# A new order for one core: DeltaNet attention and a GELU MLP, the same operations listed in another sequence

## The chip, the cores and the metric

The kernel runs on one core of a Trainium2 chip. The metric is the device time of one execution in microseconds, smaller being better. The five engines work through queues of their own: TensorE (PE; its weight loads are shown as PEld), VectorE (DVE), ScalarE (ACT), GpSimd (POOL) and SyncE (SP). SP computes nothing and issues most of the DMAs.

## The reference

A linear attention with the delta rule, over 4 batches and 8 heads with 768 tokens of 48 values, and a two-layer MLP on its output:

```python
k_n = k / (norm(k) + 1e-6)
for t in range(768):                       # per batch and head, state is 48x48
    y[t] = q[t] @ state
    v_old = k_n[t] @ state
    state = state + beta[t] * outer(k_n[t], v[t] - v_old)
x = y as (3072 tokens, 384)
h = x @ w_in                               # 384 -> 2048
out = gelu_tanh(h) @ w_out                 # 2048 -> 384
```

Inputs and outputs are float32; the kernel computes in bf16 with float32 sums.

## The kernel before

**Chunks.** The 768 tokens are cut into 12 chunks of 64 (c = 0 to 11). In a chunk the recurrence is a triangular system of 64 equations per batch and head, and its inverse is built by matrix products. A chunk has two units (u = 2c and 2c + 1), each of two batches on the two halves of the 128 partitions and 8 heads.

**Names.** Each operation is recorded by `A(engines, name, function, ...)` under a name such as `rt2.13`: the step, then the chunk or the unit.

- `load` (L422 to 433): k, q and v of a chunk by four DMAs each (`k5.01`), into one of three buffers; all but the first are on SP.
- `norms` (from L445): `sq`, `sum`, `pow`, `eps`, `nsq` or `nsa`, `inv`, `ib` give beta over the squared norm of k.
- `prep` (from L469), for a unit: `kc`, `kb`, `qb` cast and scale; their transposes come by PE and a copy (`T`, `kT`; in the first units `Tc`, `Tb`, `Tk`, `Tq`) or by a DMA transpose on SP (`turn`, L510). Gram matrices (`G2`, `G`; in the first units `GM`, `GQ`) are masked by DVE into `ln` and `wp` (L525). Then five rounds i = 1 to 5 double the precision of the inverse: `A_i` (8 products, L566), `rt_i` on DVE (add twice the identity, L578), `B_i` (8 products), and the copy of the result from PSUM into the block-diagonal operand `bd` of the next round. The sum may come from the identity matmul instead (`J`, `C`, with a copy `rj`). The copy to `bd` has three forms: two copies straight from PSUM (`bde`, L338), a copy and a masked copy that can follow each other at once (`bdf`, L338 and L344), or a copy to `xi` and two copies from there (`bdc`, L608, on POOL or DVE). `X10` and `X11` make the first operand (L555 on POOL, L557 on DVE).
- `chain` (from L611): `K`, `R`, `U`, `Un`, `S`, `Sn`, `Q`, `O`, `On` apply the inverse, carry the state to the next chunk and give the chunk's output. `X` with `xT`, or a DMA transpose `turnx` (L704), transposes the output for the MLP.
- `mlp` (from L708): 16 `up` of three matmuls each (L716), a `gelu` for each four of them (L720), 2 x 4 `down` of four matmuls each (L727), the copies `Z`, and the stores `out`.
- `weights` (L435 to 443): `w1.0`, `w1.1`, `w2.0`, `w2.1`, the halves of the two weight matrices, by DMAs that POOL issues, each released by the v loads of chunk 0. `w1.0` serves `up0` to `up7`, `w1.1` the others; `w2.0` serves `down00`, `down01`, `down10`, `down11`, `w2.1` the others.
- `warm_up`: 70 matmuls on zeros (`fill`), of which the order uses 31.

**What sets the order.** A string `ORDER` holds one sequence of all operations. A word gives the name, behind a colon the engine, where there is a choice (a, d, g, s), and behind an @ the PSUM bank that the operation takes. `Flow.order` hands each engine its words in that sequence, and `Flow.emit` puts semaphore waits in for the data and for the banks. So the string decides four things: which of the alternative forms is used, on which engine an operation runs, where it stands in that engine's queue, and in which bank a result lies. POOL operations on the two halves of the partitions also wait for each other.

A chunk's prep runs ahead of its chain, and the MLP of earlier chunks stands between on PE, a few matmuls at a time. In the order before, the four weight DMAs stand together:

```python
qb.1:g X11.1:g fill47@6 A1.0@7 rt1.0 fill52@6 Tk.2@6 kTk.2:d B1.0@3 C1.1 w1.0 w1.1 w2.0 w2.1 GM.3@6 GM.2@4 kTq.0:a bde11.0:a bde10.0:d C2.0
...
kb.4:g rt3.3 fill37@5 xT.0:a up0.0@0 B3.3@5 up4.0@2 up5.0 up6.0 up7.0 bde30.3:a bde31.3:a xi3.2:d A4.3@5 rt4.3 bdc30.2:g bdc31.2:g kb.5:g
```

Of the kernel before, what the change touches and what calls it, by code (L numbers as in the profile page):

```python
# [21 lines left out]
fill46@0 J1.1@0 fill22@1 fill64@2 Tc.1@1 fill12@2 betaT0@3 fill63@4 Tc.0@2 fill60@4 fill9@5 fill56@4 sq.0b:d sum.0a sum.0b tabS pow.0a
kTc.1:a betaA010 betaA001 pow.0b betaA011 betaA000 epsb:d eps.0a:d nsq.0a:g inv.0a eps.0b:d nsa.0b inv.0b triwpm0:d bdz0:d ib.0b:d triwpm2:d
upone0 sq.1:a sum.1 ib.0a:g kb.0:g bdz1:g kb.1:g betaT1@3 Tb.0@1 kTc.0:d betaN111 betaN110 Tb.1@4 fill25@2 kTb.0:a pow.1 eps.1:g nsa.1
kTb.1:d GM.0@6 GM.1@4 J2.0@2 fill16@1 betaN101 two:d betaN100 inv.1 ib.1:g kb.2:g ln.0 kb.3:d wpm.0 ln.1 ladj16:d wpm.1 qb.0:a fill36@3
# [4 lines left out]
X10.3:g bdc30.0:g X11.2:g qb.3:g bdf20.1:a bdf21.1:a C3.1 rj3.1:a A1.3@0 GQ.1@4 fill1@1 fill45@2 wqa.1 A4.0@1 B3.1@2 fill55@3 Tq.3@3 A1.2@4  # L30
fill41@5 rt4.0 sum.2 rt1.3 B4.0@1 wqa.0 bdf30.1:a bdf31.1:a A4.1@5 fill14@0 rt4.1 B4.1@5 fill20@0 bdf40.0:a rt1.2 pow.2 bdf41.0:a bde41.1:a
A5.0@2 B1.3@4 bde40.1:d rt5.0 kTq.3:d B1.2@0 bde10.3:a xi1.2:a R0a.0:d eps.2:g bdz5:g wqb.0 A5.1@5 B5.0@2 rt5.1 kc.4:d bde11.3:d B5.1@3
bdf50.0:a qb.2:a bdc11.2:g bdc10.2:g R0b.0:g Tq.2@5 A2.2@0 bde51.1:d rt2.2 wqb.1 nsq.2:g bde50.1:a bdf51.0:a A2.3@4 U.0@2 tabG Un.0:a rt2.3
# [4 lines left out]
gelu3.0 bdf50.3:a gelu2.0 bdf51.3:a kc.7:a down00.0@2 down01.0 sum.3 turn.5 X11.4:g wp.4 vs.1:d X10.4:d G2.5@0 S.0@6 A1.4@3 v2.01 v2.10
v2.11 q3.00 q3.01 q3.10 q3.11 k4.01 k4.10 k5.10 k4.00 k4.11 down02.0 ln.5 pow.3 eps.3:g nsq.3:g Sn.0:a bde50.2:a bde51.2:a rt1.4 inv.3 G.5@0
K.1@6 wp.5 X11.5:g X10.5:g ib.3:g kb.7:g R.1 qb.7:g B1.4@3 down10.0@4 down11.0 bde11.4:a bde10.4:a A1.5@5 GQ.2@0 A2.4@3 U.1@6 down03.0 rt1.5  # L40
rt2.4 Un.1:a wpq.2 B2.4@3 B1.5@5 xi2.4:a Q.1@6 S.1@0 O.1 down12.0 qb.6:g kb.6:g Z0.0:d bdc21.4:d bdc20.4:g A3.4@3 sq.4:g bdf10.5:a Sn.1
On.1:a turn.7 bdf11.5:a X.1@2 down13.0 xT.1:a rt3.4 sum.4 A2.5@5 B3.4@3 rt2.5 up0.1@6 up1.1 G.7@0 Z1.0:a bdf30.4:a bdf31.4:a B2.5@5 up2.1
A4.4@4 G2.7@2 up3.1 turn.6 q4.00 q4.10 q4.01 out11.0 q5.10 bde21.5:a bde20.5:a gelu0.1 wp.7 rt4.4 ln.7 up8.1@0 A3.5@5 B4.4@4 up9.1 G2.6@2
G.6@6 pow.4 eps.4:g rt3.5 ln.6 nsa.4 inv.4 ib.4:d wp.6 bdf40.4:a bdf41.4:a up10.1 B3.5@5 up11.1 up4.1@2 up5.1 A5.4@4 up6.1 bdf30.5:a
bdf31.5:a X11.7:g X10.7:g A4.5@5 A1.7@6 up7.1 X10.6:d rt5.4 X11.6:g kc.9:g q4.11 rt4.5 B5.4@7 A1.6@4 kb.8:g qb.8:g k5.11 v3.01 k5.00 k5.01
gelu2.1 kc.8:a gelu1.1 xi5.4:a v3.00 q5.01 turn.8 v4.01 v3.11 vs.2:g bdc51.4:g bdc50.4:g qb.9:g sq.5:g kb.9:g q5.11 k6.01 q5.00 turn.9 k6.00
k6.10 v3.10 k6.11 rt1.7 B4.5@5 up12.1@0 up13.1 up14.1 B1.7@2 rt1.6 B1.6@4 K.2@6 bde41.5:a bde40.5:d A5.5@5 down10.1@3 bde11.7:d rt5.5
bde11.6:a bde10.6:a bde10.7:a R.2 B5.5@5 A2.6@4 up15.1 A2.7@2 down00.1@6 bdf50.5:a bdf51.5:a gelu3.1 rt2.6 rt2.7 sum.5 B2.6@7 U.2@4
bdf20.6:a Un.2:a B2.7@2 bdf20.7:d down01.1 down11.1 bdf21.6:d bdf21.7:d down12.1 G2.8@4 Q.2@0 A3.7@2 ln.8 rt3.7 A3.6@7 O.2 On.2:a S.2@4
B3.7@2 pow.5 X11.8:g eps.5:g X10.8:g bde30.7:a bde31.7:a nsa.5 down02.1 G.8@0 rt3.6 B3.6@7 Sn.2 down03.1 bde31.6:a A4.7@2 X.2@4 wp.8 inv.5  # L50
rt4.7 A1.8@5 down13.1 rt1.8 Z0.1:a bde30.6:a xT.2:a B4.7@2 A4.6@7 Z1.1:d rt4.6 G2.9@0 G.9@4 ln.9 wp.9 B1.8@3 xi4.7:a qb.10:a ib.5:g kb.11:g
qb.11:g kc.10:d kb.10:g bdc41.7:g bdc40.7:g X11.9:g vs.3:g X10.9:g bdf10.8:a bdf11.8:a up8.2@6 B4.6@2 bde41.6:a bde40.6:a up9.2 up4.2@0
up10.2 up11.2 A5.7@4 gelu2.2 up5.2 up6.2 A5.6@5 sq.6:d rt5.6 rt5.7 sum.6 up7.2 up0.2@2 K.3@6 B5.7@4 B5.6@5 R.3 k7.01 k7.00 k7.10 out11.1
k7.11 q6.01 v4.11 turn.10 q6.10 out00.0 kc.12:g kc.11:g turn.11 sq.7:g gelu1.2 up1.2 A2.8@0 up2.2 A1.9@1 up3.2 up12.2@6 up13.2 bde50.7:d
rt2.8 rt1.9 bde51.7:a bdf50.6:a bdf51.6:a U.3@4 up14.2 B2.8@0 gelu0.2 Un.3:a B1.9@1 Q.3@2 up15.2 bde11.9:a bde21.8:a gelu3.2 pow.6 eps.6:g
nsq.6:g bde10.9:d sum.7 pow.7 kc.14:g bde20.8:a O.3 On.3:d inv.6 A2.9@1 down00.2@4 ib.6:d rt2.9 down01.2 G.10@2 G2.10@6 wp.10 ln.10 down02.2
B2.9@5 down10.2@1 A3.8@0 down11.2 G2.11@6 S.3@2 rt3.8 X11.10:g X10.10:g kb.12:g ln.11 bde20.9:a kc.13:a bde21.9:a B3.8@5 bdf30.8:a bdf31.8:a
kb.13:g X10.11:g X11.11:g A3.9@0 down12.2 down13.2 k8.00 q6.00 v4.10 q6.11 qb.12:a qb.13:g turnx.3 v4.00 k8.01 k8.11 turn.12 k8.10 rt3.9
Sn.3 A4.8@5 rt4.8 B3.9@0 A1.10@6 eps.7:g vs.4:g G.11@2 down03.2 wp.11 Z0.2:d rt1.10 Z1.2:a bdf30.9:a bdf31.9:a B4.8@5 bde41.8:a bde40.8:a
up12.3@0 up13.3 A1.11@2 A4.9@3 rt4.9 up14.3 up15.3 out11.2 q7.01 turn.13 q7.00 out00.2 v5.01 v5.10 v5.00 q7.11 v6.10 q7.10 v5.11 gelu3.3  # L60
rt1.11 up0.3@6 B1.10@3 B4.9@5 A5.8@4 up1.3 K.4@0 up2.3 up3.3 bde41.9:d rt5.8 R.4 bde40.9:a bdf10.10:a A5.9@2 bdf11.10:a up4.3@4 gelu0.3
# [729 lines left out]
```

## Time and profile before

| | before |
|---|---|
| median of 3 runs (lowest, highest) | 264.64 us (262.08, 266.8) |
| span of the profiled execution | 261.9 us |
| PE matmuls, busy | 5481, 243.3 us |
| DVE, busy | 346 instructions, 208.7 us |
| ACT, busy | 305 instructions, 189.7 us |
| POOL, busy | 216 instructions, 140.6 us |
| first `up` starts | 40.1 us |
| last `down` starts | 257.6 us |

The span runs from the first to the last instruction of the profiled execution; the times of the runs also hold what lies around it, and that execution's own device time is not listed apart from them. In the rows below, a group of instructions has its line, engine, operation, tiles and shapes, the count behind an x, then the busy time and the mean of one in ns, then the idle time of the engine ahead of them and what ended it. In the chain of waits a row has its start, its length, and the engine and line. A row of a window has its bounds and length, then for each engine the busy time and its count, then the granted clock of PE, the share of the DMA engines and the GB/s. Matmuls overlap and their ends are modelled, so the distance of starts tells PE's pace better than the busy time. Line numbers are those of the kernel before; behind the order string, those of the changed kernel are lower by 6.

### The profile page before, as it was taken

To read this page: it belongs to the slowest core of one execution; us is meant where nothing else is said; L and a number is where in the kernel's file an instruction comes from. 1 tells how busy PE (TensorE), PEld (TensorE's weight loads), DVE (VectorE), ACT (ScalarE), POOL (GpSimd) and SP (SyncE) were. 2 spreads that over 40 slices of the span, in tenths; PEclk is the share of its full clock that TensorE was granted. 3 is DMA by queue.
4 is the path that set the end of the run, shared out by engine and by line. 5 is a ranking of instruction groups with operands and counts; after the bars stand their busy time and mean duration, and the time that the engine had idled before them with its cause. 6 is when DMAs were issued, how large, how long until landed. Compare 5 with 4: busy or idle time off the path is not lost.

```text
span 261.9 us, 12280 instructions
## 1 busy us (share of the span) xinstructions
PE 243.3 (93%) x5481; PEld 189.0 (72%) x5481; DVE 208.7 (80%) x346; ACT 189.7 (72%) x305; POOL 140.6 (54%) x216
## 2 busy tenths in 40 slices
PE   5788869999999899979999989999999999999994
PEld 1356657777878768857887877787977878878672
DVE  4699996998999999949998979799999878665100
ACT  4878886879969867947986866887847858856260
POOL 7668563687986998575165462669433522011000
PEclk9979999999999999989999999999999999999999
DMA  4869999789986988993768969568976611001422
GB/s 89 148 128 154 194 186 179 139 158 170 151 154 131 139 158 159 161 166 72 142 121 161 175 122 149 102 121 111 161 144 86 120 33 33 5 3 33 91 64 60
DMA packets 118741, 31.87 MB, mean 122 GB/s; under 512 B 112800, under 2 KB 117920, under 8 KB 118688
## 3 DMA queue, kind: packets, MB, share of 16 engines
...
q0 software_dynamic: 2880, 3.15, 7.3%
...
## 4 chain that ended last, share of the span: by engine, by line
PE 75%; SPq 10%; DMA 6%; DVE 5%; issue 2%; ACT 1%
PE ps L727 24%; PE ps L716 21%; PE ps L566 18%; SPq L431 10%; DMA qraw<-in_q_dram 6%; PE ps L521 4%; PE ps L639 3%; PE ps L662 2%; PE ps L687 2%; DVE wp L525 1%; PE ps L674 1%; DVE sq L454 1%; DVE tok L484 1%; DVE rl L578 1%; SPq L406 0%
## 5 line engine op out<-in xcount | busy, mean ns | idle before, releaser
L716 PE MATMUL ps<-xT,W 128*128 128x256 bf16 x576 | 77.4, 273 | 0.4 <-ACT xT L338 0.2
L338 ACT ACTIVATE bd<-ps 64x512 bf16<-64x512 f32 x108 | 62.2, 588 | 17.6 <-PE ps L566 16.3
L727 PE MATMUL ps<-W,gT 128*128 128x384 bf16 x384 | 73.2, 329 | 0.0
L720 ACT ACTIVATE gT<-ps 128x1024 bf16<-128x1024 f32 x48 | 48.4, 1020 | 12.4 <-PE ps L716 12.0
L716 PEld LDWEIGHTS ps<-xT,W 128*128 128x128 bf16 x576 | 50.1, 98 | 6.4 <-ACT xT L338 0.5
L578 DVE TENSOR_TENSOR rt<-ps,two 128x512 bf16<-128x512 f32 x68 | 45.4, 684 | 6.6 <-PE ps L566 6.0
L727 PEld LDWEIGHTS ps<-W,gT 128*128 128x128 bf16 x384 | 33.7, 98 | 18.5 <-issue 0.7
L608 POOL COPY bd<-xi 64x256 f32<-64x256 f32 x46 | 19.0, 413 | 50.3 <-ACT xi L338 44.7
L555 POOL TENSOR_SCALAR_AFFINE_SELECT bd<-ln 64x512 bf16<-64x512 bf16 x43 | 29.7, 692 | 20.3 <-DVE ln L525 15.6
L525 DVE CAST_PREDICATED wp<-mup,ps 128x1024 bf16<-128x1024 uint16 (+1 forms) x26 | 28.3, 1090 | 2.6 <-PE ps L521 2.5
L457 POOL TENSOR_TENSOR nrm<-nrm,half 128x16 f32<-128x16 f32 x9 | 26.2, 2908 | 5.7 <-DVE nrm L455 5.5
L566 PE MATMUL ps<-rt,bd 128*128 128x64 bf16 x576 | 27.9, 194 | 0.3 <-DVE rt L578 0.3
L566 PE MATMUL ps<-wp,bd 128*128 128x64 bf16 (+1 forms) x576 | 27.3, 188 | 0.7 <-POOL bd L555 0.5
L578 DVE TENSOR_TENSOR rl<-ps,two 128x384 bf16<-128x384 f32 (+1 forms) x48 | 22.9, 483 | 5.4 <-PE ps L566 4.8
L338 DVE CAST bd<-ps 64x512 bf16<-64x512 f32 x37 | 25.0, 680 | 2.5 <-PE ps L566 2.1
L566 PEld LDWEIGHTS ps<-wp,bd 128*128 128x128 bf16 x576 | 23.6, 98 | 4.3 <-POOL bd L555 0.9
L566 PEld LDWEIGHTS ps<-rt,bd 128*128 128x128 bf16 x576 | 23.2, 98 | 4.2 <-DVE rt L578 0.8
L566 PE MATMUL ps<-rl,bd 128*128 128x64 bf16 x384 | 18.5, 193 | 2.1 <-DVE rl L578 2.1
L525 DVE CAST_PREDICATED ln<-mlo,ps 128x512 bf16<-128x512 uint16 x24 | 16.3, 682 | 4.9 <-PE ps L521 4.7
L566 PE MATMUL ps<-ln,bd 128*128 128x48 bf16 (+1 forms) x384 | 18.1, 188 | 1.0 <-DVE bd L338 1.0
L338 ACT ACTIVATE xi<-ps 128x512 bf16<-128x512 f32 x24 | 14.0, 593 | 6.5 <-PE ps L566 6.3
L566 PEld LDWEIGHTS ps<-rl,bd 128*128 128x128 bf16 x384 | 15.1, 98 | 4.8 <-DVE rl L578 3.1
...
## 6 DMA issues: line engine op xcount, KB each, us to landing
qraw<-in_q_dram SPq DMA_DIRECT2D x48, 96.0 KB, 3.4
vraw<-in_v_dram SPq DMA_DIRECT2D x48, 96.0 KB, 3.2
kraw<-in_k_dram SPq DMA_DIRECT2D x44, 96.0 KB, 3.3
...
W<-in_moe_w_in_dram POOLq DMA_DIRECT2D x2, 768.0 KB, 10.6
...
kT<-tok SPq DMA_TRANSPOSE x19, 4.5
out_dram<-ob SPq DMA_DIRECT2D x3, 96.0 KB, 2.1
```

Source lines behind the costliest of these rows:

```text
L338: return e.activation(out, in_, ACT.Copy) if e is nc.scalar else e.tensor_copy(out, in_)
L431: lambda e, P, n=n, a=a, y=y, xs=xs, view=view: e.dma_start(raw[n][s][hf(a), :, :].rearrange("p (xg y) d -> p xg y d", y=2)[:, xs, y, :], ...
L457: if e is nc.scalar else e.tensor_tensor(nr[:, 1, hx], nr[:, 0, hx], half[:, hx], ALU.pow), reads=[nrn, "half"] + ["one", "roots"] * (c < ...
L521: ins = e.matmul(o, kT[s][r, y, g, hf(a)], kT[s][r, z, g, hf(a)])
L525: return e.copy_predicated(out.rearrange("p (x g) t -> p x g t", x=2), mask[:, 0:wd].bitcast(U16).unsqueeze(1).unsqueeze(1).to_broadcast([ ...
L555: A(("pool", "dve"), op(f"X1{a}"), lambda e, P, src=ln[m][hf(a), :, :], dst=bd[b_][hf(a), :, hf(a)], a=a: e.affine_select(out=dst, in_=src ...
L566: ins = e.matmul(P(name)[:, C * h + cs.start:C * h + cs.stop], bd[b_][:, h, :], rhs[:, h, cs], **kw)
L578: A(("dve",), op(f"rt{i}"), lambda e, P, i=i, cs=cs, cn=cn, r_=r_: e.tensor_tensor(r_[:, :, cs], P(ps(f"A{i}")).rearrange("p (h t) -> p h ...
L608: A(("pool", "dve"), op(f"bdc{i}{a}"), lambda e, P, src=xi[i_][hf(a), :, :], dst=bd[b_][hf(a), :, hf(a)]: e.tensor_copy(dst.bitcast(F32), ...
L716: ins = e.matmul(P(ph)[:, 256 * f:256 * f + 256].rearrange("p (x t) -> p x t", x=2), W1[:, j, 128 * (i + f):128 * (i + f) + 128], x_[:, :, ...
L720: A(("act",), f"gelu{i // 4}.{c}", lambda e, P, i=i, ph=ph: e.activation(g_[:, i:i + 4, :], P(ph).rearrange("p (f t) -> p f t", f=4), ACT. ...
L727: ins = e.matmul(P(po)[:, 0:DM], g_[:, f, 128 * b:128 * b + 128], W2[:, f, :], start=(f == 0), stop=(f == FC - 1))
```

## The change

The order string is replaced by another one. Nothing else differs. The new string has 1735 words instead of 1750, since other alternatives are chosen in places; the words whose engine is the first of the possible ones carry no letter. On each engine the sequence is new from the first instruction on.

What the new string uses, in operations:

| step | before | after |
|---|---|---|
| copies `bde` on ACT, DVE | 78, 32 | 87, 27 |
| copies `bdf` on ACT, DVE | 56, 14 | 75, 17 |
| `xi` on ACT, DVE | 24, 6 | 14, 3 |
| `bdc` on POOL, DVE | 46, 14 | 29, 5 |
| `rt` on DVE, sums by `J` and `C` | 116, 4 | 119, 1 |
| `kb` on POOL, DVE | 19, 5 | 22, 2 |
| `vs` on POOL, DVE | 8, 3 | 10, 1 |
| `sq` on POOL, DVE, ACT | 5, 3, 5 | 6, 3, 4 |
| transposes of a unit by PE, by DMA | T.4, 19 | T.5 and T.10, 18 |
| transposes of a chunk's output by PE, by DMA | 5, 7 | 6, 6 |

The start, the places of the weights, and the first users of the weights, in the diff (the words on a line are in the one sequence):

```diff
-k0x0.10:s k0x0.01:s k0x1.01:s k0x1.10:s beta00:s k1.00 k1.01 k1.10 k1.11 beta11:s q0.00 q0.01 q0.10 q0.11 v0.00 v0.01 v0.10 v0.11 wz:d
-fill23@0 tmplz:d pad0:g pad4:g tmpl0 k0x0.00:a k0x1.00:a tmpl1 fill54@1 k2.00 k2.01 k2.10 k2.11 q1.00 q1.01 q1.10 q1.11 v1.00 v1.01 v1.10
...
-qb.1:g X11.1:g fill47@6 A1.0@7 rt1.0 fill52@6 Tk.2@6 kTk.2:d B1.0@3 C1.1 w1.0 w1.1 w2.0 w2.1 GM.3@6 GM.2@4 kTq.0:a bde11.0:a bde10.0:d C2.0
...
-gelu1.0 qb.5:g qb.4:a GQ.3@6 A4.2@4 rt4.2 up1.0 B4.3@5 up2.0 B4.2@4 up3.0 up12.0@2 wpq.3 bdf40.3:d bdf41.3:d bde40.2:a bde41.2:a T.4@6
...
+k1.00 bdz3:g upone0 one ident k0x1.00:a bdz0 pad1 wz:d fill16@1 mmup:d mup0 fill12@2 half:d fill36@3 fill65@0 k0x0.10:a mmlo:d k0x1.10 mlo0
+mlo1 k1.01 k0x1.11 k0x1.01 tmplz:d pad3:g tmpl0 tmpl1 identf triln0:g k0x0.11:a ident2 k0x0.00:a fill64@2 triln1:d fill66@0 ladj32:d
+fill52@6 fill22@1 k0x0.01:a upone1 fill28@3 bdz4 two fill49@0 beta00:a fill20@1 mup1 k1.10 beta01 k1.11 pad0:g sq.0b:d sum.0b beta10 pad4:g
...
+bde41.0 A5.0@0 rt5.0 kTq.0:a bdz2:g w1.1 B4.1@5 q4.00 bde40.1 X11.2 bde41.1:d X10.2 A1.2@4 rt1.2 B1.3@1 B5.0@0 GQ.0@6 A5.1@5 rt5.1 k3.01
+bde10.3 bdf50.0 bdf51.0 B1.2@2 bdf10.2 bdf11.2 fill47@3 k3.11 k4.00 bde11.3:d q3.01 qb.4:g B5.1@4 bde50.1 bde51.1:d w1.0 ib.2:g kb.4:g
+GQ.1@0 wpq.1 pad5:g R0b.0:g fill23@3 Tq.3@5 A2.2@2 rt2.2 A2.3@3 rt2.3 v1.11 kTq.3:a wqa.0 R0a.0:g U.0@0 Un.0 fill26@4 B2.2@2 bdf20.2:d w2.0
+B2.3@3 bdf20.3 bdf21.3 fill46@4 GQ.3@6 wqb.0 O.0@0 On.0 bdf21.2:d A3.2@4 rt3.2 kc.7:g A3.3@3 q4.11 rt3.3 X.0@2 xT.0:d B3.2@4 bde30.2:d
+bde31.2:d kc.5 B3.3@5 qb.5:a kc.6:g kb.5:g up4.0@2 up8.0@0 sq.3:g up5.0 up9.0 up10.0 up11.0 up6.0 bde31.3 wpq.3 bde30.3 A4.3@5 sum.3 up0.0@6
+up1.0 up2.0 tabG turn.4 q3.11 rt4.3 B4.3@5 v1.01 A4.2@4 up7.0 w2.1 gelu2.0 up12.0@0 up13.0 bdz5:g triwpm5:g bde41.3 pow.3 up3.0 rt4.2 B4.2@4
...
+A5.2@2 rt5.2 G.5@0 wp.5 vs.1 K.1@6 R.1 B1.4@4 bdf10.4 v3.01 down01.0 kb.7:g turn.7 X10.5 B5.2@2 bdf11.4 down02.0 GQ.2@0 A2.4@3 wpq.2 rt2.4
...
```

On SP's queue the loads no longer stand four by four: those of one chunk are spread, and loads of later chunks stand between. POOL's queue has kc.7, kc.6, kb.5 and sq.3 between w2.0 and w2.1.

More of the change, by code (lines that the diff above doesn't have):

```diff
@@ L22 @@
[L22 to L25, printed above, removed]
@@ L30 @@
[L30 to L33, printed above, removed]
@@ L38 @@
[L38 to L61, printed above, removed]
@@ new lines @@
+down10.0@4 X11.5 A1.5@0 v3.10 bde50.2 rt1.5 bde51.2 U.1@6 Un.1 sq.4:g sum.4 v3.11 down03.0 Z0.0 B2.4@3 bde20.4 B1.5@2 bdf10.5:d Q.1@6
+bde21.4 O.1 S.1@0 On.1 down11.0 q4.01 Sn.1 A3.4@3 rt3.4 kb.6:g turn.6 down12.0 bdf11.5 X.1@5 xT.1:d B3.4@3 A2.5@2 rt2.5 bde30.4 pow.4
+eps.4:g nsq.4:g inv.4 ib.4:g v2.11 bde31.4 G.7@0 kb.8:g G2.7@6 ln.7 X10.7 down13.0 Z1.0 B2.5@5 wp.7 up0.1@2 up4.1@6 bde21.5 bde20.5 A4.4@4
+k5.01 up1.1 up2.1 rt4.4 up3.1 G2.6@0 ln.6 A3.5@5 B4.4@4 rt3.5 X11.7 up5.1 up6.1 up7.1 qb.9:g kc.9:g gelu0.1 X11.6 B3.5@5 bde31.5 kb.9:g
@@ new lines @@
+X10.9 qb.11:g v4.00 X11.9 up9.2 up10.2 up11.2 gelu2.2 B1.8@1 xi1.8 bdc10.8 bdc11.8 A5.7@0 rt5.7 T.10@2 kT.10 A5.6@5 v5.01 B5.7@4 rt5.6
+A1.9@0 up0.2@6 up1.2 up2.2 up3.2 rt1.9 sum.6 A2.8@5 vs.4 kc.12 up12.2@0 B5.6@2 up13.2 up14.2 bdf50.7 bdf51.7 gelu0.2 qb.13:g bde50.6:d
+up15.2 bde51.6 out11.1 B1.9@4 out11.0 turn.11 G2.11@6 rt2.8 k7.00 sq.7:d gelu3.2 G2.10@2 ln.10 v6.00 ln.11 down10.2@5 bde10.9 U.3@0 Un.3
+B2.8@2 bde21.8:d down00.2@3 pow.6 bde11.9 k8.11 eps.6:g nsq.6:g Q.3@6 G.10@0 wp.10 O.3 On.3 A2.9@4 rt2.9 down01.2 down02.2 k8.01 bde20.8
@@ new lines @@
+q10.00 k11.00 B1.16@1 bdf10.16 bdf11.16 A5.14@0 rt5.14 v7.00 q10.10 rt1.17 B3.15@4 bde30.15 down01.5 down02.5 kb.18:g B5.14@5 bde51.14
+bde31.15 A2.16@7 down10.5@0 k10.00 sq.10:g sum.10 vs.7 B1.17@1 out00.3 R.7 down11.5 bde11.17 rt2.16 bde50.14 A4.15@2 bde10.17 rt4.15
+down03.5 out11.3 Z0.5:d q10.11 qb.20:a pow.10 B2.16@3 bde20.16:d out11.4 bde21.16 B4.15@2 down12.5 bde41.15 A2.17@1 rt2.17 down13.5 A3.16@3
+rt3.16 eps.10:g nsq.10 turn.18 G2.18@6 G.18@4 bde40.15 A5.15@1 rt5.15 wp.18 Z1.5 B2.17@0 bde21.17 up8.6@2 up9.6 B3.16@1 ln.18 turn.19 up10.6
@@ new lines @@
+A5.16@4 R.8 A1.19@0 A5.17@5 up12.7@6 rt5.16 B5.16@4 bde50.16 up13.7 up14.7 rt1.19 kb.21:g Z1.6 up15.7 gelu3.7 B1.19@0 rt5.17 B5.17@5
+bdf50.17 q11.00 q11.11 B2.18@1 xi2.18 up2.7 up3.7 qb.22:g bde51.16:d up8.7@6 up9.7 up10.7 turn.20 bdf10.19:d bdf11.19:d A2.19@4 kc.21
+turn.21 kc.22:g pow.11 up4.7@0 up11.7 v9.01 bdc21.18 bdf51.17:d bdc20.18:d A3.18@5 v11.00 up5.7 rt2.19 B2.19@4 gelu0.7 U.8@2 gelu2.7
+bdf20.19 eps.11:g rt3.18 B3.18@5 xi3.18 up6.7 up7.7 bdc30.18 Un.8:d v9.11 bdf21.19 v9.10 Q.8@6 nsq.11 G2.20@2 ln.20 bdc31.18 v10.11
```

130 lines of the change are left out of this document (67 added, 63 removed).

## Prediction

> **What bounds the kernel now.** I read the page's engine shares first, then the chain of waits in order of time, then the timeline around the two ends of the prologue, then the windows in which TensorE (PE) stood still.
>
> ```profile
> PE 243.3 (93%) x5481; PEld 189.0 (72%) x5481; DVE 208.7 (80%) x346; ACT 189.7 (72%) x305; POOL 140.6 (54%) x216
> PE 75%; SPq 10%; DMA 6%; DVE 5%; issue 2%; ACT 1%
> ```
>
> PE is busy 93% of the span and three quarters of the chain is PE. DVE at 80% is the only engine near it.
>
> ```profile
> 28.97 15.54 DMA qraw<-in_q_dram
> 44.53 0.53 ACT tok L338
> 45.20 0.83 PE ps L493 x12
> 59.27 0.51 PE ps L699 x6
> 95.18 0.76 PE ps L727 x4
> 96.17 0.65 PE ps L727 x4
> 112.58 1.71 issue
> 140.73 0.47 PE ps L566 x16
> 150.69 1.05 issue
> 248.00 5.24 PE ps L716 x48
> 253.24 5.21 PE ps L727 x32
> 258.48 0.49 ACT ob L338
> ```
>
> The last rows give PE's undisturbed pace: an up of 3 matmuls takes 5.24/16 = 0.328 us, a down of 4 takes 5.21/8 = 0.651, eight 128x128 products 0.47/2 = 0.235. The same down takes 0.76 where an operation in the other array mode (64-row tiles) follows it: a change of mode costs about 0.11.
>
> ```profile
> 40.08 0.50 PE L716 MATMUL ps<-xT,W 128*128 128x256 bf16 x3 [0.22 <-ACT xT L338]
> 50.00:60.00 10.00, 9.89 (x317) 7.28 (x315) 9.46 (x16) 8.29 (x15) 8.65 (x12) 1.00 0.92 153
> 113.00:114.00 1.00, 0.00 (x0) 0.00 (x0) 0.53 (x1) 0.00 (x0) 1.00 (x1) 1.00 0.85 146
> 116.00:117.00 1.00, 1.00 (x26) 0.57 (x18) 0.56 (x2) 0.69 (x2) 0.31 (x1) 0.50 0.75 146
> ```
>
> The first up starts at 40.08, so the span has three parts. Prologue: 40.08. From the first up to the end of the last down (258.48 less some 0.04): 218.4. Tail (copy, last store): 261.9 - 258.4 = 3.5. In the middle part PE's work, each operation at its pace, is 192 ups x 0.328 = 63.0, 96 downs x 0.65 = 62.4, 209 eight-matmul products 47.6, and 28.2 for Gram, state, output and transpose matmuls at the medians of their starts: 201.2. So about 17 us of the middle part is not work. Two stalls inside one operation, released by nothing the profile shows (1.71 and 1.05), belong to no order; after the first the granted clock was 0.50 for about 3 us, which costs half of that, 1.5. That is some 4.3; the remaining 13 are short waits on copies and DMAs.
>
> **The change, part by part.** Only the order string differs. I counted both queues operation by operation.
>
> PE. The first up in the new order is up4.0. The work from it to the end is that of before with one more 12-matmul transpose (T.5 and T.10 for T.4), one more 6-matmul transpose (X.5), one product and its neighbours less: 0.67 + 0.34 - 0.26 = +0.75. Mode changes go from 96 to 92: -0.4. Sum +0.35. Three identity matmuls in the prologue become DVE adds; they stood in idle time and cost nothing either way.
>
> Engines. The evacuation of a product now goes straight into the block diagonal (bde, bdf) more often, and by way of xi and two copies (bdc) less.
>
> ```profile
> L338 ACT ACTIVATE bd<-ps 64x512 bf16<-64x512 f32 x108 | 62.2, 588 | 17.6 <-PE ps L566 16.3
> L344 ACT ACTIVATE bd<-ps,up 128x512 bf16<-128x512 f32 x26 | 17.5, 673 | 0.0
> L338 ACT ACTIVATE xi<-ps 128x512 bf16<-128x512 f32 x24 | 14.0, 593 | 6.5 <-PE ps L566 6.3
> L608 POOL COPY bd<-xi 64x256 f32<-64x256 f32 x46 | 19.0, 413 | 50.3 <-ACT xi L338 44.7
> L608 DVE COPY bd<-xi 64x256 f32<-64x256 f32 x14 | 5.1, 363 | 1.1 <-ACT xi L338 0.8
> L484 DVE TENSOR_TENSOR tok<-kraw,nrm 128x384 bf16<-128x384 f32 x5 | 5.4, 1083 | 0.0
> L454 DVE TENSOR_TENSOR sq<-kraw 128x768 f32<-128x768 f32 x1 | 2.2, 2233 | 0.0
> L454 POOL TENSOR_TENSOR sq<-kraw 128x768 f32<-128x768 f32 x5 | 7.3, 1464 | 0.9 <-DMA kraw<-in_k_dram 0.7
> L338 POOL CAST tok<-kraw 128x384 bf16<-128x384 f32 x12 | 6.0, 502 | 2.7 <-DMA kraw<-in_k_dram 1.7 <-POOL bd L555 0.9
> L484 POOL TENSOR_TENSOR tok<-kraw,nrm 128x384 bf16<-128x384 f32 x19 | 16.2, 853 | 3.3 <-PE ps L674 2.8
> ```
>
> ACT: bd 108 to 123 (+8.8), bdf's second half 26 to 39 (+8.7), xi 24 to 14 (-5.9), smaller ones by their rows -6.7: +4.9. DVE: bdc 14 to 5 (-3.3), kb 5 to 2 (-3.2), whole squares 1 to 2 (+2.2), the rest -2.1: -6.4. POOL: bdc 46 to 29 (-7.0), against more scaling of k and v, casts and presets: about +2. All three stay under PE's 243. As PE ends last, I take these shifts at nothing; the cover is PE's queue, and in the stretch 50 to 60 above it is thin, DVE 9.46 of 10. For bare latencies I laid each PE operation at its pace and asked how late its producers come if no engine queues: the shortfalls over the middle part add up to 4.0 us before and 4.7 after. Neither order is tighter than the other in that.
>
> Prologue up to the first up. The first chunk's chain, walked in the new queues with the durations of the rows (transposes, Gram, five rounds of product, add, product, copy), reaches A1.0 at about 18.1 and U.0 at 35.2; before, they lie at 18.3 and 35.3. The last leg is one that can be followed:
>
> ```profile
> L338 ACT ACTIVATE us<-ps 128x768 bf16<-128x768 f32 x11 | 8.9, 807 | 1.4 <-PE ps L662 1.3
> L538 POOL TENSOR_TENSOR wp<-wp,mup 128x512 bf16<-128x512 bf16 x2 | 2.3, 1152 | 0.0
> L338 ACT ACTIVATE xo<-ps 128x768 bf16<-128x768 f32 x10 | 8.1, 808 | 10.8 <-PE ps L687 10.7
> L338 DVE COPY xT<-ps 128x768 bf16<-128x768 bf16 x2 | 1.1, 550 | 0.1
> ```
>
> ACT has kTq.3 and wqa.0 (0.6 each) between bde50.1 and Un.0, so Un.0 (0.81) ends at 37.1 and wqb.0 on POOL (1.15 from 36.3) at 37.5; then O.0. Two copies of unit 3 (0.59 + 0.67) come ahead of On.0 on ACT, which ends at 39.2; six transposes and xT.0, now on DVE (0.55), give 40.5 for the first up, against 40.1. The start is +0.4. ACT now issues all of the first half of k, one after another, but the second half, issued by SP, is squared first and covers it.
>
> Weights. This is the step that I think decides.
>
> ```profile
> 20.08 1.77 POOL L440 DMA_DIRECT2D W<-in_moe_w_in_dram  x2
> 21.85 1.78 POOL L442 DMA_DIRECT2D W<-in_moe_w_out_dram  x2
> 22.06 12.67 SPq L431 DMA_DIRECT2D qraw<-in_q_dram  x4
> 34.77 9.02 SPq L431 DMA_DIRECT2D kraw<-in_k_dram  x4
> DMA to landing us min/median/max: 9.0/14.4/21.4
> qraw<-in_q_dram SPq DMA_DIRECT2D x48, 96.0 KB, 3.4
> ```
>
> Before, POOL issues the four weight blocks in a row from 20.08; the first lands 9.0 later, the last 21.4 after its issue at about 22.8, at 44.2: after the first, one every (44.2 - 29.1)/3 = 5.0. While they move, loads on SP's queue take 12.67 and 9.02 for four instead of some 2.7, and the q of chunk 2 lands 15.54 after issue instead of 3.4. In the new order the blocks are spread over POOL's queue. By the same walk w1.1 is issued at about 27, w1.0 at 31 behind three mask steps, w2.0 at 34.6, w2.1 only behind kc.7, kc.6, kb.5 and sq.3 (0.50 + 0.50 + 0.85 + 1.46 = 3.3), and kc.7 waits for the k of chunk 3, which SP issues at about 27.7, into the weights. w1.0 should land at 27 + 9 + 4.2 = 40.2, just as the first up wants it: no cost. w2.0 lands at 45 to 46, before the first down at 40.5 + 8.1. For k of chunk 3 the bounds are the undisturbed 3.4 (landing 31) and the 15.54 of the q load among the weights (43.2). I take 42, nearer to the upper row, as two blocks are ahead of it. Then w2.1 is issued at 45.3 and, with the 9.0 of a block that finds the queue empty, lands at 54.3. Its first user, down02.0, stands 10.9 us of PE work behind the first up, and the Gram of chunk 2 before it waits for turn.4, a DMA transpose that SP issues behind the slowed loads. So down02.0 is due at 51.4 to 52: PE stands some 2.6 us. The bounds are 0 (k lands at 31) and 4.1 (k at 43.2, w2.1 at 55.5). Queued behind it are all later PE operations, so the stall is paid in full. What the change gives back, the q of chunk 2 ahead of the weights, saves only the 0.38 that PE waited there, and turn.4 takes it again.
>
> ```profile
> 45.20 0.83 PE L493 MATMUL ps<-ident,tok 128*128 128x128 bf16 x12 [0.38 <-ACT tok L338]
> ```
>
> A PE stall can cost more than itself: the 1.71 above was followed by a clock of 0.50 for 3 us, which would add 1.5 here; a wait of 1.05 was followed by none. I leave it out of the sum and in the range. The Trainium skill (TensorE: Matmul & The Clock Gate, Part 1: The HAM clock gate) says that the clock halves after at least one idle window of about 3.4 us; by it the stall costs 2.6 and no more, by the row 4.1. The trace speaks against the rule here.
>
> Sum: 261.9 + 0.35 (PE work) + 0.4 (start) + 2.6 (w2.1) = 265.3. The three timed runs have their median 2.7 above the profiled span, and I carry that over: 264.64 + 3.4 = **268.0**.
>
> **The rivals.**
> (a) Faster: DVE's queue, not PE, makes most of the 13 us of short waits. Its place is 50 to 110, where DVE is above 9 of 10. If all of the 6.4 us that it sheds comes out on the path and w2.1 comes in time, 264.64 + 0.75 - 6.4 = 259.0. It counts as faster only if over 5.3 + 0.75 of it comes out. Against it: only 5% of the chain is DVE. 0.13.
> (b) Slower by one mechanism, the weights: k of chunk 3 lands at the upper bound, w2.1 comes 4.1 us late, the clock halves (1.5), and the v of chunk 1, behind the same loads, is late by 2: 264.64 + 0.75 + 7.6 = 273.0. It decides from 4.6 us of stalls on. 0.23.
> (c) ACT becomes the bound in the middle: its 4.9 us come out on the path, on top of 3.4: 272.9. For it: ACT waits for PE in most of its idle time, so it is just in time; against it: 72% busy. 0.12.
> (d) The change does nothing that counts: weights and loads are hidden, 264.64 + 0.75 = 265.4. 0.14.
>
> **How the numbers follow.** The forecast as summed has 0.38. Faster by over 2% (below 259.3; 2% is about what a measurement of this kernel can tell from no change) is (a) with little else: 0.14. Slower by over 2% (above 269.9) is (b), part of (c), and the clock case of the forecast: 0.36. Within: 0.50. The range runs from (a) to a little beyond (b), 259 to 276; the forecast's own is 265 to 270.
>
> **What would show it.** Right: the first up at 39 to 42; w2.1 issued after 43; PE idle 1 to 4 us ahead of a down around 52, released by the landing of W; DVE busy near 202, ACT near 195; the middle part's other idle near 17. Wrong: no wait on W at all; short waits in 50 to 110 clearly fewer (a) or, on ACT's copies, more (c); a stall inside an operation of another length than 1.71, which no order explains.

## The result, and the profile after

The changed kernel takes 273.14 us (median of 4 runs, 270.21 to 275.92), the kernel before 264.73 (4 runs, 262.08 to 266.8): ratio 1.0305, 95% interval 1.0211 to 1.0399. It is slower. Medians here and below are of all runs, and ratios leave out the slow ones, those more than 1.5% above the quickest of the same kernel. The profiled execution took 270.21 us with a span of 268.5, the quickest of its four; the span before was 261.9. Line numbers after are 6 smaller than before.

Engine shares and the head of the chain, from the page of the changed kernel:

```profile
PE 244.6 (91%) x5490; PEld 191.1 (71%) x5496; DVE 197.6 (74%) x334; ACT 195.0 (73%) x315; POOL 140.5 (52%) x206
PE 66%; DMA 11%; SPq 7%; DVE 6%; POOL 5%; issue 2%; ACT 2%; POOLq 0%; ACTq 0%
```

PE's work is what it was, DVE is 11.1 us lighter, and PE's share of the chain has fallen from 75% to 66%: what grew is DMA, POOL and DVE. The chain of waits in order of time shows where:

```profile
26.41 0.64 SPq L425
27.08 13.79 DMA kraw<-in_k_dram
40.92 0.96 POOL tok L332 x2
41.88 0.79 POOL tok L478
42.67 1.44 POOL sq L448
44.13 0.95 DVE nrm L449
45.09 0.48 DVE rl L572
45.61 0.80 PE ps L560 x16
```

Read it from the bottom. PE starts B4.3 at 45.61, as soon as DVE has made rt4.3 (L572). DVE was free, but its queue had sum.3 (L449) ahead of rt4.3, and sum.3 reads sq.3, which POOL makes behind kc.7, kc.6 and kb.5, and kc.7 reads the k of chunk 3, whose last load takes 13.79 us where such a load takes 3.4 by the median. The timeline of the changed kernel has the three engines standing one behind another (start, length, engine, in brackets the idle time before and what ended it):

```profile
40.92 0.96 POOL L332 CAST tok<-kraw 128x384 bf16<-128x384 f32 x2 [5.71 <-DMA kraw<-in_k_dram]
44.04 0.94 POOL L436 DMA_DIRECT2D W<-in_moe_w_out_dram  x1
...
44.13 0.95 DVE L449 TENSOR_REDUCE nrm<-sq 128x16 f32<-128x768 f32 x1 [2.52 <-POOL sq L448]
...
45.61 0.48 PE L560 MATMUL ps<-rl,bd 128*128 128x64 bf16 x8 [2.33 <-DVE rl L572]
...
88.35 0.53 PE L515 MATMUL ps<-kT 48*64 48x64 bf16 x16 [0.98 <-DMA kT<-tok]
98.43 0.49 PE L515 MATMUL ps<-kT 48*64 48x64 bf16 x32 [1.81 <-DMA kT<-tok]
```

The last two rows are a second loss, at Gram matrices that wait for DMA transposes (turn.9 and turn.11). The windows (PE's busy time first, the granted clock third from the end) hold both, first the changed kernel, then the kernel before:

```profile
40.00:58.00 18.00, 15.21 (x307) 11.54 (x304) 11.59 (x19) 12.37 (x19) 14.82 (x20) 0.91 1.13 162
78.00:98.00 20.00, 17.15 (x422) 14.12 (x420) 15.51 (x24) 16.38 (x27) 15.12 (x18) 1.00 0.88 150
...
45.00:47.00 2.00, 1.39 (x20) 1.19 (x21) 1.10 (x4) 0.59 (x1) 2.00 (x3) 0.70 0.64 129
47.00:49.00 2.00, 2.00 (x15) 1.41 (x13) 0.59 (x2) 1.02 (x1) 1.97 (x1) 0.50 1.35 210
49.00:50.00 1.00, 1.00 (x27) 1.00 (x25) 0.40 (x1) 0.99 (x2) 0.42 (x2) 0.90 1.28 192
```

```profile
40.00:58.00 18.00, 17.54 (x476) 13.97 (x476) 15.32 (x25) 13.57 (x22) 10.96 (x17) 1.00 0.90 153
78.00:98.00 20.00, 19.05 (x475) 14.91 (x475) 19.12 (x28) 16.88 (x28) 17.21 (x22) 1.00 0.84 144
```

The wait of 2.33 is followed by some 3.4 us at half the clock (that is what 0.70, 0.50 and 0.90 in the three short windows add up to), and PE does 307 matmuls in the first stretch where it did 476. To put sizes to this I took each PE operation's start to the next one's start, less the pace of its kind in the trace of before, and summed the rest by stretch (us):

| | before | after | after_small_w | clear_of_weights | clear_and_v3_early |
|---|---|---|---|---|---|
| first up starts | 40.08 | 39.62 | 37.96 | 39.88 | 40.54 |
| lost, 40 to 60 | 1.7 | 6.1 | 2.3 | 3.0 | 3.2 |
| lost, 60 to 80 | 1.6 | 1.2 | 1.3 | 1.5 | 1.7 |
| lost, 80 to 110 | 2.7 | 7.0 | 3.9 | 4.7 | 2.0 |
| lost, 110 to 160 | 7.8 | 4.8 | 4.2 | 5.0 | 4.7 |
| lost, from 160 | 2.9 | 3.7 | 4.6 | 3.7 | 3.9 |
| last `down` starts | 257.63 | 263.76 | 255.49 | 259.89 | 257.87 |

(The three columns on the right are kernels of the next section.) The 6.1 us between the first two columns is +4.4 early, +4.3 at 80 to 110, +0.5 of work (what the losses leave of the time behind the first up) and +0.4 elsewhere, less 0.5 at the start and 3.0 at 110 to 160, where the kernel before has its two stalls inside an operation and the half clock.

### The profile page after: what moved, and what is told of

Same layout as the page of the kernel before. It is cut to its first block, busy times and chain, and to the rows that moved or that the text cites. A ratio compares the mean times of both kernels' runs of the same rounds, so it can differ in the third digit from the quotient of the medians.

```text
span 268.5 us, 12276 instructions
## 1 busy us (share of the span) xinstructions
PE 244.6 (91%) x5490; PEld 191.1 (71%) x5496; DVE 197.6 (74%) x334; ACT 195.0 (73%) x315; POOL 140.5 (52%) x206
## 3 DMA queue, kind: packets, MB, share of 16 engines
q1 hardware_dynamic: 111584, 26.90, 57.5%
q0 software_dynamic: 2880, 3.15, 7.0%
## 4 chain that ended last, share of the span: by engine, by line
PE 66%; DMA 11%; SPq 7%; DVE 6%; POOL 5%; issue 2%; ACT 2%; POOLq 0%; ACTq 0%
PE ps L721 20%; PE ps L710 19%; PE ps L560 15%; DMA kraw<-in_k_dram 8%; SPq L425 6%; PE ps L515 3%; PE ps L633 3%; DMA kT<-tok 2%; PE ps L681 1%; PE ps L656 1%; DVE wp L519 1%; DVE ln L519 1%; DMA vraw<-in_v_dram 1%; POOL nrm L451 1%; DVE nrm L449 1%
## 5 line engine op out<-in xcount | busy, mean ns | idle before, releaser
L332 ACT ACTIVATE bd<-ps 64x512 bf16<-64x512 f32 x123 | 71.6, 588 | 26.1 <-PE ps L560 24.2
L721 PE MATMUL ps<-W,gT 128*128 128x384 bf16 x384 | 74.2, 328 | 0.4 <-issue 0.4
L710 PEld LDWEIGHTS ps<-xT,W 128*128 128x128 bf16 x576 | 51.5, 99 | 7.5 <-issue 0.6
L572 DVE TENSOR_TENSOR rt<-ps,two 128x512 bf16<-128x512 f32 x71 | 48.1, 685 | 10.1 <-PE ps L560 9.6
L549 POOL TENSOR_SCALAR_AFFINE_SELECT bd<-ln 64x512 bf16<-64x512 bf16 x41 | 27.2, 662 | 25.2 <-DVE ln L519 21.9
L572 DVE TENSOR_TENSOR rl<-ps,two 128x384 bf16<-128x384 f32 (+1 forms) x48 | 23.0, 484 | 9.2 <-PE ps L560 8.6
L338 ACT ACTIVATE bd<-ps,up 128x512 bf16<-128x512 f32 x39 | 26.1, 674 | 2.0 <-DVE bd L332 2.0
L560 PEld LDWEIGHTS ps<-wp,bd 128*128 128x128 bf16 x576 | 21.8, 97 | 6.3 <-DVE wp L519 2.3
L602 POOL COPY bd<-xi 64x256 f32<-64x256 f32 x29 | 11.7, 406 | 25.1 <-ACT xi L332 21.8
L478 POOL TENSOR_TENSOR tok<-kraw,nrm 128x384 bf16<-128x384 f32 x22 | 18.1, 830 | 4.5 <-DVE nrm L460 3.0
L560 PEld LDWEIGHTS ps<-rl,bd 128*128 128x128 bf16 x384 | 16.1, 99 | 5.3 <-DVE rl L572 3.0
```

The lines of the kernel that those rows point to most:

```text
L332: return e.activation(out, in_, ACT.Copy) if e is nc.scalar else e.tensor_copy(out, in_)
L338: return e.activation(out, in_, ACT.Copy, scale=up1[:, 0:1]) if e is nc.scalar else e.tensor_scalar(out, in_, up1[:, 0:1], None, op0=ALU.mult)
L478: A(("dve", "pool"), op("kb"), lambda e, P: e.tensor_tensor(kb, kr, nr[:, 5, hx].unsqueeze(2).to_broadcast(full), ALU.mult), reads=[f"kraw ...
L549: A(("pool", "dve"), op(f"X1{a}"), lambda e, P, src=ln[m][hf(a), :, :], dst=bd[b_][hf(a), :, hf(a)], a=a: e.affine_select(out=dst, in_=src ...
L560: ins = e.matmul(P(name)[:, C * h + cs.start:C * h + cs.stop], bd[b_][:, h, :], rhs[:, h, cs], **kw)
L572: A(("dve",), op(f"rt{i}"), lambda e, P, i=i, cs=cs, cn=cn, r_=r_: e.tensor_tensor(r_[:, :, cs], P(ps(f"A{i}")).rearrange("p (h t) -> p h ...
```

## The experiments

Each edit only moves words of the order string, except where said. Times are medians, ratios are to the kernel before on the same chip.

**First round: the two places in the trace.** Theory one: the weights' traffic delays k of chunk 3, and DVE's queue passes that on. Theory two: from 56 us on SP issues loads with 20 us and more to spare ahead of DMA transposes. Rival: the new forms and engines, or PE's order.

k3_early, on SP's queue:

```diff
-k3.00 q2.00 q3.10 v2.00 q2.10 q3.00 v1.10 k3.10 q4.00 k3.01 k3.11 k4.00
+k3.00 k3.01 k3.10 k3.11 q2.00 q3.10 v2.00 q2.10 q3.00 v1.10 q4.00 k4.00
```

> The changed kernel with one edit: the other three k loads of chunk 3 (k3.01, k3.10, k3.11) stand right behind k3.00 on SP's queue, ahead of q2.00, so that they are on their way before the first weight block. Theory of the weights: kc.7 no longer waits 5.7 us on POOL, sq.3 and sum.3 come before rt4.3 is due, the 2.6 us gap of PE ahead of B4.3 at 42.7 and the half clock behind it go, w2.1 is issued before 40; time 4 us below the changed kernel's 273.1, so about 269, ratio to the kernel before 1.015. Theory of SP's queue (its order from 56 us on is the loss): less than 1.5 us, about 272, ratio 1.03, since the transposes of 83 to 98 us come as late as before. Theory of the forms and engines (more copies on ACT): no change, 273, ratio 1.03.

273.97 us, ratio 1.0367 (1.0293 to 1.0442): nothing gained. The wait ahead of B4.3 is gone, but q2.10 now goes out 0.3 us behind the first weight block and takes 9.5 us, and POOL stands for it, with w1.0 and the scaled v of the first chain behind it; PE waits 7.01 us for that in U.0, and the first up starts at 45.04. POOL's row and PE's, in k3_early:

```profile
35.12 0.50 POOL L332 CAST tok<-qraw 128x384 bf16<-128x384 f32 x1 [7.03 <-DMA qraw<-in_q_dram]
...
39.35 0.82 PE L656 MATMUL ps<-rs,bd 128*128 128x48 bf16 x16 [7.01 <-POOL rs L638]
```

sum3_late, the sequence cut to the words that count (bde41.3 runs on ACT, pow.3 on POOL):

```diff
-sum.3 rt4.3 bde41.3 pow.3 rt4.2
+rt4.3 bde41.3 rt4.2 sum.3 pow.3
```

> The changed kernel with one edit: sum.3 and pow.3 stand behind rt4.3 and rt4.2 on DVE's queue instead of ahead of them; loads, weights and all else stay. Theory of the weights, if DVE's queue standing behind sum.3 is what PE pays: rt4.3 runs as soon as A4.3 is done, the gap of 2.3 us ahead of B4.3 goes or shrinks below 0.8, though k of chunk 3 still lands at about 41; 269 to 271. If the lateness of k itself is what costs (v of chunk 1, k of chunk 4, w2.1 behind it): the gap goes but the time comes back before down02.0 at 56, 272 to 273. Theory of SP's queue and theory of the engines: under 1 us, 272 to 273.

270.28 us, ratio 1.0246 (1.0182 to 1.0309). The wait ahead of B4.3 goes, as theory one says of DVE's queue, and comes back one operation later. Timeline of sum3_late, POOL, DVE, PE:

```profile
43.61 0.95 POOL L332 CAST tok<-kraw 128x384 bf16<-128x384 f32 x2 [8.55 <-DMA kraw<-in_k_dram]
...
46.81 0.95 DVE L449 TENSOR_REDUCE nrm<-sq 128x16 f32<-128x768 f32 x1 [2.33 <-POOL sq L448]
...
48.41 0.36 PE L560 MATMUL ps<-wp,bd 128*128 128x32 bf16 x8 [2.98 <-DVE bd L332]
```

The time hits the 269 to 271 of theory one, but the wait that was to go has only moved, and the interval overlaps that of the changed kernel, so no gain is shown. A word moved on one queue only changes who is behind the late load.

sp_by_need and k3_early_sp_by_need: all that SP issues after 52 us in the order of first use, alone and with k3_early. On SP's queue, the part around turn.9:

```diff
-turn.8 k6.10 q6.11 v4.01 k6.11 q5.11 q5.01 k7.01 out00.0 v3.00 q6.01 turn.9
+v3.01 turn.8 v3.10 v3.11 v3.00 turn.9 v4.10 v4.01 v4.11 v4.00 q6.10 q6.11
```

> The changed kernel with one edit: the DMAs that SP issues after 52 us in the changed kernel's trace are put in the order of their first use there (a DMA transpose 2 us sooner), so that turn.8, turn.9 and turn.11 no longer stand behind loads and stores that have 20 to 40 us to spare. Theory of SP's queue: PE's waits on the DMA transposes (2.8 us by the trace's groups) go and the bubbles of PE between 80 and 110 us fall from 7.0 to about 3; time 4 us below 273.1, about 269, ratio 1.015. Theory of the weights: the 42.7 us gap stays and the later waits are only its echo, so less than 1 us, 272 to 273. Theory of the engines: 273.

> The changed kernel with both edits, the k loads of chunk 3 ahead of the weights and SP's queue by need from 52 us on. If both theories hold and add up: 273.1 - 8 = 265, ratio 1.00. If the weights alone: 269. If SP's queue alone: 269. If the forms and engines or PE's own order are what costs: 272 or more, ratio 1.03.

275.66 us, ratio 1.0439 (1.0367 to 1.0512), and 274.89, ratio 1.0404 (1.0318 to 1.0489). Neither gains. In the first, k of chunk 3 lands later still and B4.3 waits 5.27; the wait on turn.9 is gone, but turnx.3, put only 2 us ahead of its need, makes PE wait 2.49, and a wait of 2.12 on a transpose at 100 stays. In the second nothing waits for k, and PE stands for turn.4 instead, the DMA transpose of unit 4, which is issued among the weights:

```profile
52.00 0.43 PE L515 MATMUL ps<-kT 48*64 48x64 bf16 x16 [5.54 <-DMA kT<-tok]
...
41.97 7.77 SPq L504 DMA_TRANSPOSE kT<-tok  x1
```

So the single-load form of theory one falls: in these traces, whichever load is caught among the weights, something early needs it.

**Second round: take the traffic away.** after_small_w and before_small_w load one block of 128 for each half of the two matrices and let all ups and downs read it, so that seven eighths of the weights are left out of the computation:

```diff
-e.dma_start(W1[:, :, f0:f0 + FF // 2], w1v[:, :, f0:f0 + FF // 2])
+e.dma_start(W1[:, :, f0:f0 + 128], w1v[:, :, f0:f0 + 128])
-e.dma_start(W2[:, n0:n0 + FC // 2, :], w2v[:, n0:n0 + FC // 2, :])
+e.dma_start(W2[:, n0:n0 + 1, :], w2v[:, n0:n0 + 1, :])
-W1[:, j, 128 * (i + f):128 * (i + f) + 128]
+W1[:, j, 1024 * (i // 8):1024 * (i // 8) + 128]
-W2[:, f, :]
+W2[:, f // 8 * 8, :]
```

> The changed kernel with an eighth of the weights: each half of the two matrices loads one block of 128 (one row block of the second matrix) and all its ups and downs read that one, so that TensorE does the same matmuls and seven eighths of the weight traffic are left out. The computation is changed in that. Theory that the weight traffic and what it delays is the whole loss: the same edit on the kernel before gives the same time within 1%, and the changed kernel gains 7 to 10 us by it, 263 to 266. Theory that SP's later order costs 3 us besides: 266 to 269, 1% above its partner. Theory of the forms and engines or of PE's order: it stays 2 to 3% above its partner.

> The kernel before with the same eighth of the weights (seven eighths of the weight traffic left out, the same matmuls). Its first up is set by the chain of the first chunk, and the weights cost it little: 0 to 2 us, 262 to 265, by every theory. If it gains 5 us or more, the weight traffic slows the kernel before as much, and is no difference between the two.

262.91 us, ratio 1.0011 (0.9971 to 1.0052), and 262.07, ratio 0.9917 (0.9858 to 0.9976). The changed kernel gains 10.2 us, the kernel before 2.4 (the two medians against 273.14 and 264.45). What is left between them is 0.8 us by the medians and 0.9%, some 2.5 us, by the ratios. Same forms, same engines, same PE order, and most of the difference gone: it lies in what the weight traffic delays. Theory two's 266 to 269 did not come; its 1% above the partner is not ruled out by the ratios. The first windows of after_small_w:

```profile
40.00:58.00 18.00, 17.63 (x501) 13.89 (x499) 15.12 (x23) 14.75 (x24) 14.75 (x17) 1.00 0.56 81
78.00:98.00 20.00, 17.89 (x460) 14.49 (x457) 16.80 (x26) 14.69 (x24) 12.31 (x16) 1.00 0.72 129
```

In the table the stretch 80 to 110 falls from 7.0 to 3.9 with it, so some 3 us of the second loss look like an echo: SP's queue is still behind by what it lost among the weights.

after_w_together puts the weights together and earlier, with q2 and k3 ahead of them on SP. sp_turns_first is sp_by_need with the transposes 8 us ahead of need. POOL's queue in after_w_together:

```diff
-qb.3 eps.2 X11.3 bdz2 w1.1 X11.2 X10.2 qb.4 w1.0
+qb.3 w1.0 w1.1 eps.2 X11.3 bdz2 X11.2 X10.2 w2.0 w2.1 qb.4
```

> The changed kernel with the weights as the kernel before has them, and loads by need around them: w1.0 and w1.1 behind qb.3 on POOL, w2.0 and w2.1 behind X10.2 (both 2 to 14 us sooner), and on SP's queue q2 and k3 ahead of the weights, then v1, q3 and turn.4, then k4 and q4. Theory of the weights: k of chunk 3 lands before 28, the weights are all in by 49, no wait above 1 us between 40 and 58, down02.0 starts at 52 and not at 56; 273.1 - 4 = 269. Rival, that the loads are slowed by the weights wherever these stand: turn.4 lands after 50 and PE stands ahead of G2.4 as with k3 early, 273 to 275. Theory of the engines: 272 to 273.

> As SP's queue by need from 52 us on, but with the DMA transposes (turn, turnx) taken as due 8 us ahead of their first use and not 2, since the first trial left turnx.3 landing 0.04 us and turn.11 0.11 us before use. Theory of SP's queue: no wait of PE on kT or xT above 0.5 us between 60 and 160; of the 9 us of bubbles there in the changed kernel 3 go: 273.1 - 3 = 270. Otherwise 273. What happens before 58 us (the wait on k of chunk 3) should stay as it is by every theory.

270.07 us, ratio 1.0258 (1.0195 to 1.0321), and 274.04, ratio 1.0432 (1.0363 to 1.05). In the first the k load is in time, and the rival named beside it holds: turn.4 lands after 50, though 270.07 lies nearer to the 269 of the theory than to the rival's 273 to 275. Chain and timeline of after_w_together (its traced execution, 272.85, is the longest of its seven):

```profile
33.66 17.80 DMA kT<-tok
```

```profile
51.59 0.43 PE L515 MATMUL ps<-kT 48*64 48x64 bf16 x16 [4.28 <-DMA kT<-tok]
```

In the second PE is busy 19.44 us of 78 to 98, not 17.15, as theory two wants, but one wait on turn.11 of 2.03 stays beyond that (in the changed kernel most of it lies within the window, so some 1.4 us of the 2.3 have only moved out of it), k of chunk 3 lands at 43.7, and PE is busy 13.26 of 40 to 58. Nothing is left of the gain in the time.

**Third round: clear the way.** t4_on_pe gives unit 4 back to PE (T.4 and kT.4 for turn.4), T.5 behind it:

```diff
-tabG turn.4 q3.11
+tabG q3.11
...
-A5.3@5 T.5@2 rt5.3 kT.5
+A5.3@5 T.4@2 rt5.3 kT.4
...
-bdc41.2 G2.4@6 ln.4
+bdc41.2 T.5@2 G2.4@6 kT.5 ln.4
```

> The changed kernel with one choice of form undone: unit 4 is transposed by TensorE and a copy (T.4, kT.4, 12 matmuls more) as in the kernel before, and turn.4, the DMA transpose that is issued while the weights move, is gone; T.5 follows it. Theory now (what stands behind loads in flight with the weights, turn.4 and the k of chunk 3 alike): SP's queue is 5 us freer after 40, but the k of chunk 3 still lands at about 41 and sum.3 still holds DVE, so the wait ahead of B4.3 stays; 1 to 2 us less than 273.1, 271 to 272. If turn.4 alone were the cause: 267.

274.0 us, one run at 267.2 and the other five at 271.3 to 276.9, too far apart for a ratio. In the traced execution, one of the longer ones (275.06), the wait ahead of B4.3 is there, longer. The run at 267.2 is what turn.4 alone as the cause would give; it was not traced, so what this edit gains by itself is open. t4_on_pe:

```profile
44.19 0.95 POOL L332 CAST tok<-kraw 128x384 bf16<-128x384 f32 x2 [9.79 <-DMA kraw<-in_k_dram]
...
48.86 0.61 PE L560 MATMUL ps<-rl,bd 128*128 128x64 bf16 x8 [6.42 <-DVE rl L572]
```

clear_of_weights does that and puts q2 and k3 ahead of the weights, which stay where the change has them; v1 moves up behind k3, and q3, q4 and v2 move back. SP's queue:

```diff
+q1.10 q2.00 q2.10 k3.00 k3.01 k3.10 k3.11 v1.10 v1.11 v1.01 v1.00
+q3.01 q3.10 q3.00 q3.11 k4.00 k4.01 k4.11 k4.10 q4.00 q4.11 q4.10 v2.00
```

> The changed kernel with T.4 on TensorE in place of turn.4, and q of chunk 2 and k of chunk 3 ahead of the weights on SP's queue (then v1, q3, k4, q4); the weights stay where the change has them. Nothing that PE needs before 53 us is then in flight with the weights. Theory of loads in flight: no wait above 1 us between 40 and 56, down02.0 at 51 to 52 (56.2 in the changed kernel), about 5 us off, and the later waits shrink as SP is no longer behind: 266 to 268, ratio 1.01. If the weights' places are the cost in themselves (w2.1 late): down02.0 later than 54 behind a wait on W, 270 or more.

266.32 us (265.25 to 267.73), ratio 1.0128 (1.0069 to 1.0188). No wait above 1 us between 40 and 56. Together the edits take off 6.8 us by the medians, which are of different chips, and 1.8% (some 4.7 us) by the ratios. k3 early alone had gained nothing, but it had left q2 among the weights; q2 and k3 early with turn.4 kept and the weights left in place was not run. The traces fit theory one, widened from one load to all that is in flight with the weights and needed before 53 us. down02.0 starts at 53.9, not 52; the first up comes at 39.88 behind a stall of its own (below).

```profile
40.00:58.00 18.00, 16.58 (x396) 13.23 (x394) 14.98 (x23) 13.78 (x22) 11.42 (x14) 1.00 1.03 158
78.00:98.00 20.00, 16.93 (x443) 13.68 (x442) 15.31 (x24) 15.56 (x25) 15.14 (x21) 1.00 0.95 154
```

before_w_spread is the mirror: the kernel before, with the weights spread on POOL's queue.

```diff
-w1.0 w1.1 w2.0 w2.1 X11.3 kc.5 X10.3 bdc30.0 X11.2 qb.3
+X11.3 kc.5 X10.3 w1.0 bdc30.0 X11.2 qb.3 w1.1
...
-bdc10.2 R0b.0
+bdc10.2 w2.0 R0b.0
...
-kb.5 qb.5
+kb.5 w2.1 qb.5
```

> The kernel before with its four weight DMAs spread over POOL's queue about where the change issues them: w1.0 behind X10.3 (26), w1.1 behind qb.3 (29), w2.0 behind bdc10.2 (34), w2.1 behind kb.5 (43). Theory of the prediction (the spreading as such costs): w2.1 lands at 51 to 54 and down02.0 waits up to 2.6 us, 266 to 269. Theory of loads in flight: q of chunk 2 and k of chunk 3, which in this order nothing needs before 44, land sooner, and the time stays within 1% of 264.6.

266.57 us, ratio 1.0107 (1.0045 to 1.0168): between the two. q2 and k3 land early, as the theory of loads in flight says, but w2.1 is now in flight with turn.5, and PE waits for that:

```profile
54.96 0.32 PE L521 MATMUL ps<-kT 48*64 48x64 bf16 x16 [2.49 <-DMA kT<-tok]
...
45.49 3.29 SPq L510 DMA_TRANSPOSE kT<-tok  x1
```

In the kernel before, turn.5 is issued at 45.09 in 1.71 us, when the weights are in, and lands at 49.08; here it lands at 54.8. The spreading does cost, some 2.4 us, which is near the 2.6 predicted, but PE does not wait for W, and the wait on turn.5 is not all of it. The first up starts 1.5 us later than in the kernel before, with the clock at half from 36 to 42, and the stall of 1.71 of the kernel before does not come; the two traces do not tell which of these belong to the spreading. before_w_spread:

```profile
38.00:40.00 2.00, 1.69 (x48) 1.32 (x46) 1.63 (x5) 1.38 (x2) 1.20 (x4) 0.50 1.30 214
...
41.57 0.85 PE L716 MATMUL ps<-xT,W 128*128 128x256 bf16 x3 [0.22 <-ACT xT L338]
```

clear_and_v3_early takes clear_of_weights and mends SP's queue at one place:

```diff
-k6.10 q6.11 v4.01 k6.11 q5.11 q5.01 k7.01 out00.0 v3.00 q6.01 turn.9
+k6.10 k6.11 q5.11 q5.01 v3.00 turn.9 q6.11 v4.01 k7.01 out00.0 q6.01
-v4.00 v5.01 out11.1 out11.0 turn.11 k7.00
+v4.00 k7.00 turn.11 v5.01 out11.1 out11.0
```

> The kernel clear_of_weights with one more edit on SP's queue: v3.00 (which landed 0.07 us before vs.3, after POOL had stood 2.6 us) and turn.9 go ahead of q6.11, v4.01, k7.01 and out00.0, and turn.11 ahead of v5.01, out11.1 and out11.0. Theory that SP's order is a second loss of its own: the waits of PE ahead of G2.9 (0.60), G2.11 (1.76) and B2.8 (0.95) fall to 1 us together, and the time by 1.5 to 2 us, 264.5 to 265, ratio to the kernel before 1.005. Theory that it was only an echo of the weights and is spent by now: under 0.7 us, 265.7 to 266.3.

263.58 us (12 runs, 262.08 to 264.5), ratio 0.9992 (0.9961 to 1.0023), an interval below that of clear_of_weights: theory two is a second loss of its own, 1.4% by the ratios and 2.7 us by the medians. sp_turns_first, with the first one still there, had not shown it. Waits of PE on transposes fall from 2.8 in the changed kernel and 1.9 in clear_of_weights to

```profile
PE ps L515 <- DMA kT<-tok: 0.6, 1, 0.6
```

Nothing beats the kernel before; this order draws level with it. It has the changed kernel's forms and engines but for unit 4, so these cost nothing that can be seen.

## Why the prediction was right or wrong

- The range held the time; the forecast of 268.0, within 2%, did not: the time lies above its own 265 to 270 and the kernel is slower. That the range held is partly luck: it has no term for the second loss, and 3.0 us of stalls that did not come again made up for most of that.
- PE's work (+0.35): right; about +0.5 by the table.
- The start (+0.4): first up predicted at 40.5, measured 39.62, and that with a stall of 1.46 in U.0 that was not foreseen. Without it some 38.2: the walk put U.0 at 35.2, it came at 33.30.
- The weights: the landings were right. k of chunk 3 was put at 42 and landed at 40.9 in this execution (43.6 to 44.1 in four of the experiments); w2.1 was put at 45.3 to 54.3 and ran from 44.04 to 52.05.
- **The step that failed is the next: "PE stands some 2.6 us" ahead of down02.0, for W.** I followed POOL's queue behind kc.7 only to w2.1. Ahead of w2.1 stands sq.3, and sq.3 has a follower on another engine: sum.3, in front of rt4.3 on DVE. So PE stood at 45.6 and not at 52. down02.0 came at 56.27, some 4 us after w2.1 had landed. The size, 2.33 of idle, was near the 2.6 by chance.
- The clock, left out of the sum with 1.5: it was paid. With it, the stretch from 40 to 60 lost 4.4 us more than before, and not 2.6.
- "The middle part's other idle near 17": wrong, 22.8 lost after the first up against 16.7. The second loss, at 80 to 110, had no step in the prediction; SP's order past 56 us was not walked. clear_and_v3_early gives the size of what it mends: 266.32 to 263.58.
- The stalls of the kernel before were carried over as belonging to no order; 3.0 us at 110 to 160 did not come again, which hid part of the loss. One of the two does belong to the order: the 1.05 comes in all three traces that keep the order before on PE, at the same matmul (last section).
- The 2.7 between the profiled span and the median was too small: it is 4.6 here. The profiled execution is the quickest of four, 2.9 below their median, and its span is 1.7 below its own time.
- Rivals. (a) DVE shed 11.1 us, not 6.4, and none of it can be seen in the time: with most of the weights left out the changed order is still 0.8 to 2.5 us behind its partner. (b), the weights at 273.0, is the case that came, by its cause; w2.1 and v of chunk 1 were not what PE waited for, and as it lacks the second loss, that it lies so near to 273.14 is chance. (c) ACT is at 195.0 as counted, and after_small_w has that load at 262.91, so it does not bound. (d) falls.

Of the announced signs, the first up, w2.1's issue and ACT held; the wait on W did not come, DVE is at 197.6 and not 202. A stall inside an operation of another length than 1.71, named as a sign of being wrong, did come, 1.46 in U.0. POOL, counted at 5 us less, came out as before (140.5).

Open: why k of chunk 3 lands at 40.9 in one execution and near 44 in others of nearly the same queue, and why the stall of 1.71 did not return.
